# A gated mix of local attention and a spectral filter: the first unit copied from PSUM to its tiles, a third fold, the exchange in all groups but one, four odd rows unfolded on GpSimd, and another way to the order

## The chip, the cores and the metric

The kernel runs on one core of a Trainium2 chip. The metric is the device time of one execution in microseconds (us), as the median of several runs. "PE" in the profile is TensorE (matmul), "PEld" its weight loads, "DVE" VectorE, "ACT" ScalarE, "POOL" GpSimd and "SP" SyncE, which here only issues DMAs.

## The reference, cut to what matters

```python
def _A_ref(x, wqkv, wo):               # x: 1 x 2048 x 640, 32 heads of 20
    W, dil = 8, 2                      # each position looks at itself and 7 earlier ones, two apart
    qkv = (x @ wqkv)...                # q, k, v
    idx = pos[:, None] - (jnp.arange(W) * dil)[None, :]
    logits = einsum("bhsd,bhswd->bhsw", q, kg) * scale   # kg, vg: k, v gathered at idx
    logits = where(idx >= 0, logits, -1e9)
    attn = softmax(logits)
    o = einsum("bhsw,bhswd->bhsd", attn, vg)
    return o @ wo
def _B_ref(x, w_r, w_i):
    X = rfft2(x) * (w_r + 1j * w_i)
    return irfft2(X, s=(2048, 640))

g = sigmoid((x * gate_w).sum(-1))
return g * a + (1 - g) * b             # a from _A_ref, b from _B_ref, both of A_x
```

All arrays are float32; the output is 1 x 2048 x 640.

## The kernel before, in words

Position s is 16 p + j: the partition p is one of 128, and the 16 rows j are worked one at a time. As the dilation is 2, even j and odd j never meet in the attention.

**Attention.** `x` and `wqkv` are split into a high and a low float32r part, and three products of them give q, k and v for one row j and a quarter of the heads (`qkv`, 15 matmuls of 480 columns into a PSUM bank). A unit u = 4·par + hg is one parity and one quarter; unit 0 is the first. Unit 0 also carries the gate column. `qkv_first` computes seven of its eight rows with the loop over the five blocks of the contraction outside; `store` takes a finished bank: ScalarE copies it to one of two `ev` tiles, and each two rows go from there to a DRAM buffer, `qkvd`. `attend` (a unit has two halves, `a` and `b`) loads `kt` and `vt` (15 rows, of which the first 7 are the last 7 of the partition ahead) and `q` back from it. VectorE multiplies k by q (`pr`; q is first copied to a third of a PSUM bank, `qbank`, by ScalarE, so that the product has one input in SBUF and one in PSUM) and sums it to the logits `L`; GpSimd forms the products with v (`pv`), VectorE sums them (`o`), and they go to DRAM, `od`. `zero_rows` writes the zero rows ahead of position 0 into `qkvd`.

**Spectral part.** `fold` adds and subtracts mirrored columns of `x` twice on VectorE (tile `fx`, with `fe` for the even half), so that the transform along the 640 columns needs cosines or sines of a half or a quarter of them. Pairs of rows q = 2 to 7 are parked in DRAM (`fd`) by a DMA from GpSimd's queue. `cols` transforms along the partitions with matmuls into `zg`. `freq(g)`, once for each of 16 groups g of frequencies, copies from `zg` (`zc`), applies the folded transform of the columns with the table `bt` (`v` and `u`, six matmuls), adds and subtracts (`ab`), transforms over j (`x`, `z`), and multiplies by the complex weights `wp`. For that product the two halves of the partitions must change places. In the groups of `EXCHANGED` (1 to 8) ScalarE scales `x` and `z` by a sign into `X`, and two DMAs put them into the other half of `P`; in the others two more matmuls (`ix`, `iz`) compute them. GpSimd multiplies `P` by `wp` and adds, VectorE forms `s`, and matmuls (`g`) go back over j into `zg`. `spatial(j)` transforms back (`oa`, `ob`, `ha`, `hb`).

**Output.** `project_even` and `project_odd` multiply the attention's output by `wo` (transposes `oTp`, high and low parts `oT`, 15 matmuls each for `woa` and `wob`). For even j the result is parked in DRAM (`ad`) and added by GpSimd to `spatial`'s `y`. For odd j `project_odd` unfolds the spectral part (`ye`, then `y`: five instructions, on VectorE, or on GpSimd for j in `ODD_POOL`) and adds the projection to it; these projections stand last. They need `o` of every odd unit.

**The order.** Every operation is recorded by a planner, not issued at once (so all instructions carry one line, L636 in the program's own count, and are told apart by their tiles). The planner gives each a cost, runs a list schedule forwards and backwards in turn (`turns`, six times), and then tries 60 random shifts of the due times. Each resulting order is scored by its mean end under three draws of random delays (`late`), and the best one is issued as the fixed order of each engine. The queues then run by semaphores alone, each in its order. SyncE's and ScalarE's queues carry the loads and stores (`queue`: `vt` and `q` on ScalarE).

Of the kernel before, what the change touches and what calls it, by code (L numbers as in the profile page):

```python
# [16 lines left out]
S, D = 2048, 640  # L17
# [7 lines left out]
PERM = np.array([0, 320] + list(range(2, 320, 2)) + list(range(1, 320, 2)))  # L25
# [6 lines left out]
def dft_tables():  # L32
# [18 lines left out]
    def half(n, *ends):  # L51
# [3 lines left out]

    bt = np.zeros((640, 642))
    bt[0:161, 0:161] = np.cos(tau * np.outer(np.arange(161), ke) / D) * half(161, 0, 160)
    bt[161:321, 161:321] = np.cos(tau * np.outer(np.arange(160), ko) / D) * half(160, 0)
    bt[321:480, 323:482] = -np.sin(tau * np.outer(np.arange(1, 160), kb) / D)
    bt[480:640, 482:642] = -np.sin(tau * np.outer(np.arange(1, 161), ko) / D) * half(160, 159)  # L60
    bt = np.concatenate(
        [bt[0:128, 0:161], bt[128:256, 0:321], bt[256:384, 161:482], bt[384:512, 321:642], bt[512:640, 482:642]], 1
# [94 lines left out]
class Plan:  # L157
# [119 lines left out]
    def order(self):  # L277
# [20 lines left out]
        rng = np.random.default_rng(SEED)  # L298
        self.draws = [rng.exponential(size=len(ops)).tolist() for _ in range(DRAWS)]
        best = self.turns(TURNS)  # L300

        names = {n: i for i, n in enumerate(dict.fromkeys(op.of for op in ops))}
        family = np.array([names[op.of] for op in ops])
# [6 lines left out]
        self.ends = best[0], best[3]  # L310
# [5 lines left out]
    def turns(self, n):  # L316

        runs = []
        for i in range(n + 1):
            tails = np.array([op.tail for op in self.ops])  # L320
            done = self.forward()
            end = max(op.end + op.lat for op in done)
            runs.append((end, tails, [(op, op.start, op.end) for op in done]))
            if i < n:
                self.backward(end)
        end, tails, order = min(runs, key=lambda r: r[0])
        ends = [self.late([o[0] for o in order], d) for d in self.draws] or [end]
        return sum(ends) / len(ends), tails, order, end

    def late(self, order, draw):  # L330

        line = {e: [op for op in order if op.eng == e] for e in ENGS}
        at, free, rings, link = dict.fromkeys(ENGS, 0), dict.fromkeys(ENGS, 0.0), dict.fromkeys(ENGS, 0.0), 0.0
        over, out = {}, {}
        head = {}
        last = 0.0
        for _ in range(len(order)):
            for e in ENGS:
                if head.get(e) is None and at[e] < len(line[e]):
                    op = line[e][at[e]]  # L340
                    t = free[e]
                    for q in op.preds:
                        if q not in out:
                            break
                        t = max(t, over[q] if q.eng == e and not q.size else out[q])
                    else:
                        head[e] = t
            e = min((h for h in ENGS if head.get(h) is not None), key=lambda h: head[h])
            op, t = line[e][at[e]], head.pop(e)
            late = draw[op.i]  # L350
            if op.two and free["POOL"] > t:
                t = min(free["POOL"], t + WAIT)
            busy = op.busy * (1 + 0.015 * late) if e in ("DVE", "ACT", "POOL") and not op.size else op.busy
            over[op] = free[e] = end = t + busy
            if op.size:
                link = max(link, end) + op.size / RATE
                own = rings[e] = max(rings[e], end) + op.size / QUEUE
                end = (own if own >= link else min(link, own + op.size / QUEUE)) + SOONEST + LATER_BY * late
            else:
                end += op.lat - LATE.get(op.chain, 0.0)  # L360
            out[op] = end
            last = max(last, end)
            at[e] += 1
        return last
# [106 lines left out]
TURNS, AGAIN, MOVE, SEED = 6, 60, 2.0, 3  # L471
DRAWS, SOONEST, LATER_BY = 3, 2.4, 0.6
# [31 lines left out]
class Mixer:  # L504
# [64 lines left out]
    def work(self):  # L569
# [10 lines left out]
        self.zero_rows()  # L580
        self.qkv_first()
# [22 lines left out]
        S.dma_start(self.bt[:, 0:1284], ins["t_bt"])  # L604
# [36 lines left out]
    def zero_rows(self):  # L641
        p, d = self.p, self.qkv_d
        zero = self.one("zero", 7 * HC, tag="pv0")[0:32]
# [4 lines left out]
                offset=d.offset + 2 * ROWS * HC,  # L648
                ap=[[6 * ROWS * HC, 8], [ROWS * HC, 4], [1, 7 * HC]],
            ),  # L650
            zero,
        )

# [113 lines left out]
    def attend(self, par, h, step=4):  # L767
# [12 lines left out]
        kt, vt = (self.kvr.next(f"{i}t{nm}", 15, HC) for i in "kv")  # L780
        q = self.qr.next(f"q{nm}", 8, HC)
# [444 lines left out]
```

## Time and profile before

| | |
|---|---|
| times of three runs | 459.76, 459.97, 461.55 us |
| median | 459.97 us |
| the profiled execution | span 461.8 us from the first to the last instruction; the page has no other time for it |
| TensorE matmul / weight load | 448.4 us (97%) / 394.7 us (85%) |
| VectorE | 418.1 us (91%) |
| ScalarE | 209.7 us (45%) |
| GpSimd | 324.7 us (70%) |
| DMA | 108.53 MB, mean 235 GB/s |
| granted TensorE clock | 1.000 |

Busy shares are means over stages with different limits; what an edit is worth is read from the stage it lies in. Matmuls are pipelined and their ends are modelled, so a TensorE that reads as fully busy is not TensorE at its peak. Idle time of an engine that is not the bound costs nothing. A wait for several semaphores is put down to the one that came last.

### The profile page before, as it was taken

What the parts mean: (1) busy time and instruction counts of PE and PEld (TensorE: products, weight loads), DVE (VectorE), ACT (ScalarE), POOL (GpSimd) and SP (SyncE); (2) the same over time, 40 slices, a digit from 0 to 9 for tenths busy, and PEclk for the clock granted to TensorE, in tenths of its full rate; (3) what the DMA queues carried; (4) which work ended last, traced back from release to release, by engine and by line L of the source; (5) the groups of instructions that cost most, each with busy time, mean ns of one, the idle gap of its engine ahead of it and who ended that gap; (6) DMA issues with size and microseconds to landing.
All of it is one profiled execution on the core that took longest, in us unless ns stands there. A gap on an engine that the chain in (4) does not pass through costs nothing. (4 is left out here: it accounts for less than half of the span.)

```text
span 461.8 us, 7229 instructions
## 1 busy us (share of the span) xinstructions
PE 448.4 (97%) x2468; PEld 394.7 (85%) x2468; DVE 418.1 (91%) x549; ACT 209.7 (45%) x551; POOL 324.7 (70%) x264
## 2 busy tenths in 40 slices
PE   8999999999999989999998988999999999999996
PEld 6888888888888888898886877988889999988996
DVE  4999729999999999999989999999999997799594
ACT  4534245544235553265457665655445554432120
POOL 1003545999999879989898997797877889862200
PEclk9999999999999999999999999999999999999999
DMA  8999989769858989767989698786463321356722
GB/s 318 393 399 304 354 327 345 237 206 342 253 183 232 297 252 327 245 182 281 333 225 286 229 324 254 213 261 229 118 186 96 112 72 58 119 174 174 258 89 114
DMA packets 72836, 108.53 MB, mean 235 GB/s; under 512 B 21072, under 2 KB 50768, under 8 KB 72800
## 3 DMA queue, kind: packets, MB, share of 16 engines
q1 hardware_dynamic: 40192, 69.40, 46.8%
q10 hardware_dynamic: 31696, 34.67, 23.9%
q0 software_dynamic: 912, 4.00, 2.2%
q8 instruction: 19, 0.31, 0.3%
q14 instruction: 17, 0.14, 0.1%
HBM read 72.59 MB, written 32.84 MB: 228 GB/s over the span
## 5 line engine op out<-in xcount | busy, mean ns | idle before, releaser
L636 PE MATMUL qkv<-w,xo 128*128 128x480 f32 (+1 forms) x480 | 109.9, 384 | 0.0
L636 PE MATMUL qkv<-w,xe 128*128 128x480 f32 (+1 forms) x474 | 104.4, 381 | 1.1 <-ACT xe L636 1.1
L636 PEld LDWEIGHTS qkv<-w,xe 128*128 128x128 f32 x474 | 89.2, 188 | 16.7 <-ACT xe L636 2.2
L636 PEld LDWEIGHTS qkv<-w,xo 128*128 128x128 f32 x480 | 89.6, 189 | 13.7 <-ACT ev L636 0.2
L636 ACT COPY ev<-qkv 128x480 f32<-128x480 f32 x64 | 34.9, 556 | 38.3 <-PE qkv L636 18.7
L636 PE MATMUL woa<-wo,oT 128*128 128x320 f32 x240 | 51.5, 316 | 0.6 <-ACT oT L636 0.6
L636 PE MATMUL wob<-wo,oT 128*128 128x320 f32 x240 | 51.5, 316 | 0.0
L636 PEld LDWEIGHTS woa<-wo,oT 128*128 128x128 f32 x240 | 39.1, 188 | 1.1 <-ACT oT L636 0.8
L636 PEld LDWEIGHTS wob<-wo,oT 128*128 128x128 f32 x240 | 39.2, 188 | 0.7
L636 POOL TENSOR_TENSOR P<-P,wp 128x963 f32<-128x963 f32 (+1 forms) x16 | 30.4, 1900 | 11.8 <-ACT P L636 7.2
L636 POOL TENSOR_TENSOR w<-raw,w 128x480 fp32r<-128x480 f32 (+1 forms) x20 | 25.2, 1277 | 18.7 <-ACT w L636 18.7
L636 POOL DMA_DIRECT2D fd<-fx x6 | 4.3, 717 | 33.5 <-DVE fx L636 33.5
L636 ACT CAST oT<-oTp 128x384 fp32r<-128x384 f32 (+1 forms) x32 | 13.2, 427 | 30.4 <-PE oTp L636 26.0
L636 PEld LDWEIGHTS g<-mm,s 128*128 128x128 f32 x150 | 21.6, 190 | 3.5 <-ACT zg L636 0.5
L636 POOL TENSOR_TENSOR yi<-yi,y 128x640 f32<-128x640 f32 x8 | 12.5, 1563 | 16.8 <-DMA yi<-ad 9.6
L636 PE MATMUL v<-bt,zc 128*128 128x321 f32 (+2 forms) x96 | 22.2, 347 | 1.7 <-ACT vs L636 1.7
L636 PE MATMUL g<-mm,s 128*128 128x128 f32 x150 | 23.2, 276 | 0.0
L636 PE MATMUL oa<-gt,zg 128*128 128x161 f32 (+1 forms) x96 | 22.9, 344 | 0.0
L636 DVE TENSOR_TENSOR oT<-oTp,oT 128x384 fp32r<-128x384 f32 (+1 forms) x32 | 15.2, 483 | 8.4 <-ACT oT L636 8.4
L636 PE MATMUL ob<-gt,zg 128*128 128x161 f32 (+1 forms) x96 | 22.3, 344 | 0.0
L636 PE MATMUL u<-bt,zc 128*128 128x321 f32 (+2 forms) x96 | 22.0, 344 | 0.0
L636 ACT CAST w<-raw 128x480 fp32r<-128x480 f32 (+1 forms) x30 | 17.0, 592 | 8.0 <-PE qkv L636 2.9
(303 smaller groups left out, 1102.9 us busy)
## 6 DMA issues: line engine op xcount, KB each, us to landing
qkvd<-ev ACTq DMA_DIRECT2D x32, 480.0 KB, 5.1
wp<-in_ws SPq DMA_DIRECT2D x16, 642.0 KB, 4.9
raw<-in_wqkv SPq DMA_DIRECT2D x25, 240.0 KB, 7.0
fx<-in_x SPq DMA_DIRECT2D x8, 641.0 KB, 9.8
ot<-od SPq DMA_DIRECT2D x16, 320.0 KB, 3.3
fd<-fx POOLq DMA_DIRECT2D x6, 640.0 KB, 7.3
f<-fd SPq DMA_DIRECT2D x6, 640.0 KB, 7.1
P<-X ACTq DMA_DIRECT2D x16, 160.5 KB, 4.6
```

The lines of the kernel that those rows point to most:

```text
L636: p.dve.memset(w, 0.0)
```

## The change

Six things change together.

1. **Unit 0 is not sent through DRAM.** `open_near` takes its six tiles (q, k, v of both halves) at the start and clears the seven rows of partition 0. `store` copies each bank in six pieces of 80 columns straight into them, on ScalarE (`NEAR_DVE` is empty), and after the last row four DMAs on SyncE's queue copy the seven rows of the partition ahead within each k and v tile. `attend` then loads nothing for unit 0.
2. **Rows are folded a third time.** The even half and the odd half of what `fold` makes are folded again where this is possible, with four instructions of about 160 elements on GpSimd (`THIRD_DVE` is empty) for each of eight pairs of rows. The tables `bt` and the order of the columns `PERM` follow, and three blocks of `v` and `u` in `freq` become narrower.
3. **`EXCHANGED` goes from groups 1 to 8 to groups 1 to 15**; g = 0 keeps its matmuls.
4. **`ODD_POOL` goes from empty to (1, 3, 5, 7)**: the five unfolding instructions of these rows are on GpSimd.
5. **The search for an order is replaced.** A fixed list of 28 seeds is applied in turn: each seed shifts the due times by drawn amounts, `turns(2)` runs, and its result is taken for the next.
6. **The scoring under random delays goes**; `turns` keeps the order with the earliest end of its own schedule.

```diff
-PERM = np.array([0, 320] + list(range(2, 320, 2)) + list(range(1, 320, 2)))
+PERM = np.array([0, 320] + list(range(4, 320, 4)) + list(range(2, 320, 4)) + list(range(1, 320, 2)))
...
-        for _ in range(AGAIN):
-            move = MOVE * rng.choice([0.3, 1.0, 2.0]) * rng.normal(size=len(names))
-            move *= rng.random(len(names)) < rng.choice([0.1, 0.5, 1.0])
-            for op, t in zip(ops, (best[1] + move[family]).tolist()):
+        for seed in FOUND:
+            for op, t in zip(ops, (best[1] + self.move(seed)).tolist()):
                 op.tail = t
-            best = min(best, self.turns(2), key=lambda b: b[0])
+            best = self.turns(2)
...
-        end, tails, order = min(runs, key=lambda r: r[0])
-        ends = [self.late([o[0] for o in order], d) for d in self.draws] or [end]
-        return sum(ends) / len(ends), tails, order, end
...
+        return min(runs, key=lambda r: r[0])
+
+    def move(self, seed):
+        rng = np.random.default_rng(seed)
+        n, kind = self.kinds[rng.integers(3)]
+        shift = rng.choice([0.6, 2.0, 6.0, 15.0]) * rng.normal(size=n)
+        return (shift * (rng.random(n) < rng.choice([0.03, 0.1, 0.4, 1.0])))[kind]
...
+    def open_near(self):
+
+        self.near = [None] * 6
+        for f in range(2):
+            for i in (1, 2):
+                t = self.near[2 * i + f] = self.kvr.next(f"{'qkv'[i]}t0{'ab'[f]}", 15, HC)
+                self.p.pool.memset(t[0:1, 0:7], 0.0)
+            self.near[f] = self.qr.next(f"q0{'ab'[f]}", 8, HC)
...
         u, j = 4 * par + hg, 2 * jj + par
+        if u == 0:
+            for i, t in enumerate(self.near):
+                (p.dve if i in NEAR_DVE else p.act).copy(t[:, jj + (7 if i > 1 else 0)], b[:, HC * i : HC * i + HC])
+            p.act.copy(self.z[:, j : j + 1], b[:, 480:481])
+            if jj == 7:
+                for t in self.near[2:]:
+                    self.queue("halo").dma_start(t[1:128, 0:7], t[0:127, 8:15])
+            return
...
-        G.tensor_sub(f[:, :, 321:480], o[:, :, 1:160], o[:, :, 319:160:-1])
-        G.tensor_add(f[:, :, 480:640], o[:, :, 1:161], o[:, :, 319:159:-1])
-        G.tensor_add(f[:, :, 0:161], e[:, :, 0:161], e[:, :, 320:159:-1])
+        H = p.dve if q in THIRD_DVE else p.pool
+        G.tensor_add(f[:, :, 321:481], o[:, :, 1:161], o[:, :, 319:159:-1])
+        G.tensor_sub(o[:, :, 1:160], o[:, :, 1:160], o[:, :, 319:160:-1])
         G.tensor_sub(f[:, :, 161:321], e[:, :, 0:160], e[:, :, 320:160:-1])
+        G.tensor_add(e[:, :, 0:161], e[:, :, 0:161], e[:, :, 320:159:-1])
+        H.tensor_add(f[:, :, 481:561], o[:, :, 1:81], o[:, :, 159:79:-1])
+        H.tensor_sub(f[:, :, 561:640], o[:, :, 1:80], o[:, :, 159:80:-1])
+        H.tensor_add(f[:, :, 0:81], e[:, :, 0:81], e[:, :, 160:79:-1])
+        H.tensor_sub(f[:, :, 81:161], e[:, :, 0:80], e[:, :, 160:80:-1])
...
-        row(v, 4, bt[:, 803:1124], True, False)
-        row(v[:, 0:161], 3, bt[:, 642:803], False, False)
-        row(v[:, 161:321], 5, bt[:, 1124:1284], False, True)
+        row(v[:, 81:321], 4, bt[:, 721:961], True, False)
+        row(v[:, 161:321], 3, bt[:, 561:721], False, False)
+        row(v[:, 0:161], 5, bt[:, 961:1122], False, True)
...
-        row(u, 1, bt[:, 161:482], True, False)
+        row(u[:, 81:321], 1, bt[:, 161:401], True, False)
         row(u[:, 0:161], 0, bt[:, 0:161], False, False)
-        row(u[:, 161:321], 2, bt[:, 482:642], False, True)
+        row(u[:, 161:321], 2, bt[:, 401:561], False, True)
...
-ODD_POOL = ()
+ODD_POOL = (1, 3, 5, 7)
...
-EXCHANGED = tuple(range(1, 9))
+EXCHANGED = (1, 2, 3, 4, 5, 6, 7, 8, 9, 10, 11, 12, 13, 14, 15)
```

More of the change, by code (lines that the diff above doesn't have):

```diff
@@ L325, in turns @@
                 self.backward(end)
-        end, tails, order = min(runs, key=lambda r: r[0])
-        ends = [self.late([o[0] for o in order], d) for d in self.draws] or [end]
-        return sum(ends) / len(ends), tails, order, end
[L330 to L364, printed above, removed]
+        return min(runs, key=lambda r: r[0])
[4 more added lines that the diff above has]
+        return (shift * (rng.random(n) < rng.choice([0.03, 0.1, 0.4, 1.0])))[kind]
     @staticmethod
@@ L642, in zero_rows @@
         p, d = self.p, self.qkv_d
[L643 removed]
+        zero = self.one("zero", 7 * HC, tag="pv0")[0:28]
         p.pool.memset(zero, 0.0)
@@ L779, in attend @@
         p.chain = "logits"
-        kt, vt = (self.kvr.next(f"{i}t{nm}", 15, HC) for i in "kv")
-        q = self.qr.next(f"q{nm}", 8, HC)
-        self.queue("kt").dma_start(kt.rearrange("p a b -> p (a b)"), rows(1, 0, 15))
-        self.queue("q").dma_start(q.rearrange("p a b -> p (a b)"), rows(0, 7, 8))
-        self.queue("vt").dma_start(vt.rearrange("p a b -> p (a b)"), rows(2, 0, 15))
+        if u == 0:
+            q, kt, vt = (self.near[2 * i + f] for i in range(3))
+        else:
+            kt, vt = (self.kvr.next(f"{i}t{nm}", 15, HC) for i in "kv")
+            q = self.qr.next(f"q{nm}", 8, HC)
+            self.queue("kt").dma_start(kt.rearrange("p a b -> p (a b)"), rows(1, 0, 15))
+            self.queue("q").dma_start(q.rearrange("p a b -> p (a b)"), rows(0, 7, 8))
+            self.queue("vt").dma_start(vt.rearrange("p a b -> p (a b)"), rows(2, 0, 15))
         L = self.Lr.next(f"L{nm}", 8, 4, 8)
```

43 lines of the change are left out of this document (28 added, 15 removed).

## The prediction

> **What bounds the kernel now.** I read the page first, then the busy time by stretches, then the chain of work that ended last, then the waits, and at the end the timeline of the first 70 us.
>
> ```profile
> span 461.8 us, 7229 instructions
> PE 448.4 (97%) x2468; PEld 394.7 (85%) x2468; DVE 418.1 (91%) x549; ACT 209.7 (45%) x551; POOL 324.7 (70%) x264
> ```
>
> The profiled span is 461.8 us; the median of the three runs is 459.97. The sum below is made on the span, and the difference, 1.8 us, comes off at the end. Two engines are near full. The stretches (window, its length, then busy us and instructions of PE, PEld, DVE, ACT and POOL, then granted clock, DMA share and GB/s) show when:
>
> ```profile
> 40.00:60.00 20.00, 20.00 (x94) 17.33 (x93) 14.89 (x17) 6.75 (x14) 9.06 (x8) 1.00 0.99 337
> 60.00:80.00 20.00, 20.00 (x93) 17.28 (x92) 13.54 (x11) 10.45 (x27) 10.77 (x9) 1.00 0.94 323
> 80.00:180.00 100.00, 98.80 (x491) 86.21 (x490) 98.48 (x87) 44.98 (x115) 93.06 (x74) 1.00 0.83 259
> 180.00:280.00 100.00, 96.17 (x514) 81.97 (x513) 97.28 (x112) 53.20 (x156) 92.28 (x75) 1.00 0.84 262
> 280.00:380.00 100.00, 98.44 (x609) 87.19 (x609) 97.98 (x134) 54.21 (x151) 80.49 (x64) 1.00 0.57 172
> 414.00:462.00 48.00, 43.20 (x300) 42.07 (x298) 35.02 (x86) 8.15 (x20) 6.30 (x4) 1.00 0.50 160
> ```
>
> From 80 to 380 us TensorE and VectorE are both at 96 to 99% of the time, with the clock granted in full. Work taken off one of them alone moves little, because the other holds the end. VectorE has its one large hole ahead of that, at 40 to 80 us: 5.1 and 6.5 us idle. The chain that ended last (start, us, what) tells how the two take turns:
>
> ```profile
> 287.26 1.09 PE u L636 x6
> 300.63 0.54 PE ix L636 x2
> ...
> 412.10 1.48 DVE o4b L636
> ...
> 417.76 0.45 PE oTp L636 x2
> ...
> 456.31 2.06 PE wob L636 x14
> 458.39 0.55 DVE y L636
> ```
>
> Nearly all of its pieces between 284 and 402 us are matmuls; then VectorE finishes the last attention unit (`o4b`, over at 413.6); behind it stand the odd rows' projections, which need that output, some 40 us of matmul from 418 to 458. So the end is "last `o4b` plus 48 us", and `o4b` comes early only if VectorE's work before it shrinks and TensorE's does too.
>
> **The change part by part.** *TensorE.* The third fold narrows the row transforms: `v` and `u` write 240+160+161 = 561 columns for each group instead of 321+161+160 = 642. Six pieces of `u` take 1.09 us for 642 columns, so 81 columns are 0.138 us; over 2 outputs and 16 groups, 4.4 us. With all groups but g = 0 exchanged, the `ix` and `iz` products of groups 9 to 15 go: 14 of 0.54 us, 7.6 us. Nothing is added. TensorE: **-12.0 us**, all ahead of the last 100 us, in the full stretches.
>
> *VectorE, the first unit.* Today unit 0 goes from PSUM to `ev`, to DRAM, and back:
>
> ```profile
> DVE pr0a L636 <- ACT qbank L636: 10.9, 2, 8.7
> ACT ev L636 <- DMA qkvd<-ev: 18.2, 5, 7.0
> ```
> ```profile
> 37.96 1.02 ACT L636 COPY ev<-qkv 128x480 f32<-128x480 f32 x2 [2.02 <-DMA qkvd<-ev]
> 51.35 1.49 DVE L636 TENSOR_TENSOR pr0a<-kt0a,qbank 128x1280 f32<-128x1280 f32 x1 [2.17 <-ACT qbank L636]
> 63.40 0.56 ACT L636 COPY ev<-qkv 128x480 f32<-128x480 f32 x1 [6.99 <-DMA qkvd<-ev]
> 65.99 1.49 DVE L636 TENSOR_TENSOR pr0a<-kt0a,qbank 128x1280 f32<-128x1280 f32 x1 [8.72 <-ACT qbank L636]
> ```
> ```profile
> kt0a<-qkvd SPq DMA_DIRECT2D x1, 600.0 KB, 5.6
> vt0a<-qkvd ACTq DMA_DIRECT2D x1, 600.0 KB, 16.1
> P<-X ACTq DMA_DIRECT2D x16, 160.5 KB, 4.6
> ```
>
> Unit 0's last copies run from 37.96 to 39.0; its first product starts at 51.35. With the tiles filled straight from PSUM only seven halo rows go by DMA. Their landing is not in this trace. The nearest rows bound it: 4.6 us (the exchange, between SBUF tiles too) and 16.1 (`vt0a`, the slow one of the early loads); I take 5.6, that of `kt0a`, which is issued in the same stretch. Attention can then start at 39 + 5.6, about 45 us, with folds to fill VectorE until then, and it has q at hand when today it stops for 8.7 us. I count both waits as gone: -10.9 us. The other end is -2.2: the 8.7 us stay, because ScalarE serves in order and the `qbank` copies stood behind an `ev` copy of the next unit, which waited 6.99 us for a store, and those stores remain. For the wait going speaks that unit 0's traffic leaves DMA engines that were 94 to 99% busy just then. Late next is VectorE itself. The four halo copies stand on SP's queue and wait for the eighth bank; the later weight loads queue behind them, and TensorE needs those by the start of the next set only, so their lead hides the wait; without it, TensorE loses what the weights are late. The four memsets on GpSimd lie in its idle first 20 us.
>
> Six copies of 80 columns a bank instead of one of 480 lie between 166 ns (one column) and 556 (480 columns); linear in the width that is 0.23 us, and 48 x 0.23 - 8 x 0.556 = 6.6 us more for ScalarE. It is busy 6.75 of 20 us there, and a bank takes TensorE 15 matmuls of 20.00/94 us, 3.2 us, against 1.6 us of copies. Hidden; if ScalarE ran late, TensorE would wait for banks.
>
> ```profile
> L636 ACT COPY z<-qkv 128x1 f32<-128x1 f32 x16 | 2.5, 166 | 3.0 <-PE qkv L636 2.0 <-ACT ev L636 0.9
> L636 ACT COPY ev<-qkv 128x480 f32<-128x480 f32 x64 | 34.9, 556 | 38.3 <-PE qkv L636 18.7 <-DMA qkvd<-ev 18.2 <-issue 0.5
> L636 DVE TENSOR_TENSOR iz<-iz,wp 128x321 f32<-128x321 f32 x8 | 3.9, 493 | 0.9 <-PE iz L636 0.9
> L636 POOL TENSOR_TENSOR P<-P 128x321 f32<-128x321 f32 x16 | 12.0, 751 | 1.2
> L636 DVE TENSOR_TENSOR ye<-ho 128x160 f32<-128x160 f32 (+1 forms) x24 | 10.1, 474 | 0.2
> L636 DVE TENSOR_TENSOR y<-ye 128x321 f32<-128x321 f32 (+1 forms) x16 | 7.3, 485 | 0.1
> ```
>
> *The exchange in seven more groups.* VectorE drops one product of 0.49 us in each: -3.4 us. GpSimd multiplies three parts instead of two, about 0.75 us more each, 5.3 us. ScalarE scales twice and issues two DMAs where it made one copy, beside its 45 to 54%. GpSimd's product now waits for a landing of 4.6 us, with `pv` products queued behind it. The spacing of `s`, the last product of a group, prices that:
>
> ```profile
> 249.71 0.87 DVE L636 TENSOR_TENSOR s<-P,z 128x321 f32<-128x321 f32 x2
> 303.34 0.89 DVE L636 TENSOR_TENSOR s<-P,z 128x321 f32<-128x321 f32 x2
> 306.77 0.49 DVE L636 TENSOR_TENSOR s<-P,iz 128x321 f32<-128x321 f32 x1
> 344.39 0.89 DVE L636 TENSOR_TENSOR s<-P,iz 128x321 f32<-128x321 f32 x2
> ```
>
> Groups with the exchange (g = 0 among them) came every 53.6/8 = 6.7 us, the last seven, without, every 37.6/6 = 6.3. So it costs up to 0.4 x 7 = 3 us, or nothing if VectorE paces both. I take nothing and keep the 3 us for the range.
>
> *Third fold and odd unfolding on GpSimd.* 32 more instructions of some 160 elements, at half of the 0.75 us of 321: 0.4 us each, 13 us, mostly before 80 us, where GpSimd is half idle. The odd unfolding takes half of 10.1 + 7.3 us off VectorE, 8.7 us, nearly all behind 414, where VectorE is busy 35 of 48 us: it covers nothing there and I count nothing. But two engines meet here:
>
> ```profile
> 43.32 4.58 POOL L636 TENSOR_TENSOR w<-raw,w 128x480 fp32r<-128x480 f32 x3 [5.10 <-ACT w L636]
> 43.53 4.71 DVE L636 TENSOR_TENSOR fx<-fx 128x642 f32<-128x642 f32 x3
> L636 DVE TENSOR_TENSOR fe<-fx 128x642 f32<-128x642 f32 x8 | 6.6, 823 | 0.1
> L636 DVE TENSOR_TENSOR fx<-fx x24: 482/494/1844, 19.4 to 46.7; 128x642 f32<-128x642 f32 x8, 128x320 f32<-128x320 f32 x8, 128x318 f32<-128x318 f32 x8
> ```
>
> Three fold instructions, both inputs in SBUF, took 4.71 us while GpSimd subtracted; at the median 0.49 for the two short ones, and the 0.82 of `fe` for the wide one, they are 1.8. VectorE lost 2.9 us beside 4.58 us of GpSimd, 0.6 for one. The new thirds run beside folds, or beside attention products, whose q lies in PSUM. Bounds: nothing (all beside attention) and 13 us (each blocks a fold for its whole time). With half of them beside folds, 13 x 0.6 / 2: **+4 us**.
>
> [...]
>
> *Sum.* VectorE up to `o4b`: -10.9 - 3.4 + 4 = -10.3; TensorE -12.0; the smaller gain binds. 461.8 - 10.3 = 451.5 us of span, less 1.8: **449.7 us**. With the lock at nothing TensorE's 12.0 binds, 448.0; with the exchange's 3 us, 452.7.
>
> **Rivals.** *The replayed order closes gaps* (0.15): TensorE and VectorE each leave 6 to 7 us idle in 80 to 380, and TensorE 4.8 behind 414. An order that recovers half of the one and the other, 5 us, gives 444.7; all of it about 439.
>
> *The first unit's wait goes in part* (0.10): half of the 8.7 us stay, 454.0. *It stays whole* (0.07), the change then not doing what it says: 449.7 + 8.7 = 458.4. The ordered ScalarE speaks for it, the lighter DMA against.
>
> *The lock at full length* (0.03): 13 us instead of 4, 458.7. Against it: most folds can run before any third is ready.
>
> *Slower: an order that counts on punctual landings* (0.15). The change drops the scoring of an order under drawn delays, replays fixed draws, and adds 14 exchange DMAs whose landings an in-order GpSimd, over 90% busy, must wait for. This trace has one such case: an `ev` copy stood 6.99 us behind a store, and VectorE lost 8.72. Behind 80 us nothing absorbs it. It decides once the loss passes the 10.3 of gain and 2.3 more; two stops of 8.72 give 449.7 + 17.4 = 467.1.
>
> **How the numbers follow.** The forecast has 0.50, 448 to 453 us by itself. 0.5% is 2.3 us, about what a measurement of this kernel can tell. Faster than 457.7: 0.50 + 0.15 + 0.10 = 0.75; within: 0.07 + 0.03 = 0.10; slower: 0.15. The range for 8 in 10 runs from 441, most of the closed gaps, to 460, which takes in the wait that stays and the full lock and leaves out the slower case.
>
> **What would show it.** Right: `v` and `u` near 0.95 us for six pieces and no `ix`, `iz` but for g = 0; VectorE over 95% busy from 20 us on, the first `pr0a` near 45 us with no long wait after it; fold instructions stretched beside GpSimd by about 4 us in all; last `o4b` near 403 and 48 us behind it. Wrong: VectorE idle over 5 us before 80; GpSimd waiting for `P<-X` by more than 1 us a group; `o4b` early but matmuls left over, so that more than 48 us follow it; or new waits of TensorE on banks or weights in the first 120 us.

## The result and the profile after

The changed kernel takes **499.51 us** (median of 4 runs, 497.20 to 499.86) against 460.76 us for the kernel before on the same chip: 1.081 times as long, with an interval of 1.078 to 1.085. It is 38.8 us slower where 10.3 us less were forecast, and outside the range of 441 to 460. The profiled execution took 497.2 us, its span is 495.4.

The page after (the span, the busy time of the engines, and three rows of the 40 slices, 12.4 us each):

```profile
span 495.4 us, 7309 instructions
...
PE 449.1 (91%) x2440; PEld 396.0 (80%) x2440; DVE 414.8 (84%) x522; ACT 215.3 (43%) x598; POOL 366.7 (74%) x320
...
PE   8999908879999449999999989999998999999996
...
DVE  3999705069989999999999899999999998879484
...
PEclk9999966979999959999999999999999999999999
```

There is a hole that the kernel before did not have: TensorE at 0 in the sixth slice, VectorE at 0 in the sixth and the eighth, and a granted clock of 6 tenths in the sixth and seventh. Two shorter stops of TensorE follow in the fourteenth and fifteenth. The stretches put numbers on it (columns as in the prediction: length, then PE, PEld, DVE, ACT, POOL, granted clock, DMA share, GB/s):

```profile
60.00:80.00 20.00, 6.59 (x21) 4.29 (x19) 5.23 (x4) 1.87 (x4) 4.65 (x7) 0.63 0.31 110
80.00:100.00 20.00, 16.72 (x72) 13.88 (x70) 1.94 (x2) 0.30 (x1) 0.14 (x1) 0.93 0.18 59
100.00:180.00 80.00, 65.39 (x298) 56.09 (x298) 74.29 (x63) 34.61 (x91) 69.94 (x55) 0.91 0.77 248
```

In 60 to 80 us TensorE works 6.6 of 20 us, VectorE 5.2, and the DMA engines, which stood at 0.94 in the same stretch before, are at 0.31. Nobody is busy, so everybody waits. The timeline of SP's queue (start, time that SP spent in the issue) shows a first reason; its last line is from the kernel before:

```profile
38.88 0.73 SPq L616 DMA_DIRECT2D kt0b<-kt0b  x1
39.70 7.11 SPq L616 DMA_DIRECT2D kt0a<-kt0a  x1
46.91 15.80 SPq L616 DMA_DIRECT2D vt0b<-vt0b  x1
62.80 14.55 SPq L616 DMA_DIRECT2D vt0a<-vt0a  x1
77.45 22.46 SPq L616 DMA_DIRECT2D raw<-in_wqkv  x5
```
```profile
45.25 12.82 SPq L636 DMA_DIRECT2D raw<-in_wqkv  x5
```

These are the four halo copies, seven rows of 127 partitions each. SP is held in their issue for 38 us, from 38.9 to 77.4, and the next set's weights (`raw`) get their turn only at 77.45; before, SP issued them at 45.25. The waits (total, times, longest) and the timeline of ScalarE and TensorE (start, length, in brackets the idle time before and what ended it) show what came of it:

```profile
ACT w L616 <- DMA raw<-in_wqkv: 24.5, 3, 20.8
DVE pr0a L616 <- ACT qbank L616: 21.1, 1, 21.1
DVE pr0a L616 <- DMA kt0a<-kt0a: 15.4, 1, 15.4
PEld qkv L616 <- ACT w L616: 14.3, 2, 13.7
```
```profile
74.65 0.37 ACTq L616 DMA_DIRECT2D qkvd<-ev  x1
75.11 0.59 ACT L616 CAST w<-raw 128x480 fp32r<-128x480 f32 x1 [20.95 <-DMA kt0a<-kt0a]
75.75 20.96 PE L616 MATMUL qkv<-w,xe 128*128 128x480 f32 x79 [13.28 <-ACT w L616]
99.70 1.75 ACT L616 CAST w<-raw 128x480 fp32r<-128x480 f32 x3 [20.85 <-DMA raw<-in_wqkv]
```

VectorE waits 15.4 us for the halo of `kt0a`, until 74.67 us, 35 us after its issue. ScalarE stands twice. Its first stop, from 54.2 to 74.6 us, ends with the same landing: its next operation is a store of `ev`, which needs nothing of `kt0a`, but in the trace that store waits for semaphore 100, on which the halo copy counts its landing, and then counts its own on it. TensorE's longest wait for weights `w`, 13.3 us, ends one step behind this stop, at 75.75 us, before SP has issued the late `raw` at all. ScalarE's second stop, 20.85 us, is the wait for that `raw`. TensorE loses 5.6 us behind it, and VectorE waits 21.1 us for its q in `qbank`: in ScalarE's order that copy comes behind the cast to `w`, which starts only at 99.70 us. So the late landings reach the engines by two ways, through SP's held queue and through a store on ScalarE's queue. The first attention product starts at 74.7 us instead of 51.4, and the last `qkv` matmul ends at 282.0 instead of 242.1.

### The profile page after: what moved, and what is told of

Same layout as the page of the kernel before. It is cut to its first block, busy times and chain, and to the rows that moved or that the text cites. A ratio compares the mean times of both kernels' runs of the same rounds, so it can differ in the third digit from the quotient of the medians.

```text
span 495.4 us, 7309 instructions
## 1 busy us (share of the span) xinstructions
PE 449.1 (91%) x2440; PEld 396.0 (80%) x2440; DVE 414.8 (84%) x522; ACT 215.3 (43%) x598; POOL 366.7 (74%) x320
## 5 line engine op out<-in xcount | busy, mean ns | idle before, releaser
L616 PE MATMUL qkv<-w,xe 128*128 128x480 f32 (+1 forms) x474 | 111.4, 395 | 19.6 <-ACT w L616 13.3
L616 PE MATMUL qkv<-w,xo 128*128 128x480 f32 (+1 forms) x480 | 119.9, 394 | 7.2 <-ACT ev L616 7.1
L616 PEld LDWEIGHTS qkv<-w,xe 128*128 128x128 f32 x474 | 91.9, 196 | 38.6 <-ACT w L616 14.3
L616 ACT COPY ev<-qkv 128x480 f32<-128x480 f32 x56 | 30.9, 556 | 49.7 <-PE qkv L616 42.4
L616 PE MATMUL woa<-wo,oT 128*128 128x320 f32 x240 | 47.7, 321 | 0.1
L616 PE MATMUL wob<-wo,oT 128*128 128x320 f32 x240 | 47.0, 318 | 0.4 <-ACT oT L616 0.3
L616 POOL TENSOR_TENSOR P<-P,wp 128x963 f32<-128x963 f32 (+1 forms) x16 | 35.4, 2210 | 8.4 <-DMA P<-X 8.4
L616 PEld LDWEIGHTS woa<-wo,oT 128*128 128x128 f32 x240 | 38.8, 193 | 0.5 <-DVE oT L616 0.4
L616 DVE TENSOR_TENSOR pr0a<-kt0a,qbank 128x1280 f32<-128x1280 f32 x4 | 5.9, 1486 | 36.6 <-ACT qbank L616 21.1
L616 POOL TENSOR_TENSOR fx<-fx 128x160 f32<-128x160 f32 (+1 forms) x16 | 11.5, 735 | 23.7 <-DMA fx<-in_x 17.3
L616 PE MATMUL v<-bt,zc 128*128 128x240 f32 (+2 forms) x96 | 20.0, 323 | 1.1 <-ACT vs L616 1.1
L616 PE MATMUL u<-bt,zc 128*128 128x240 f32 (+2 forms) x96 | 18.9, 322 | 1.2 <-DVE ab L616 1.2
```

The source lines that it names most:

```text
L616: p.dve.memset(w, 0.0)
```

## Experiments: the halo copies

**Fewer rows to a copy** (`halo_split`). The changed kernel in its own order; each copy is issued as two (this edit and those below are shown in short):

```diff
-    dma_start(t[1:128, 0:7], t[0:127, 8:15])
+    dma_start(t[1:113, 0:7], t[0:112, 8:15])
+    dma_start(t[113:128, 0:7], t[112:127, 8:15])
```

> The changed kernel in its own order, but each of the four halo copies issued as two, of 112 and of 15 partitions, in place of one of 127. Theory H (a copy of 127 partitions runs on few DMA engines, and everything queued behind it waits): the hole from 62 to 102 us goes, no halo issue on SP takes over 2 us, and the time falls from 499.5 by some 35 to 45 us, to 450 to 465. Rival O (the replayed order, the lock and the exchange cost most of it): the hole shrinks but the time stays over 480.

Measured: **462.49 us** (10 runs, 459.63 to 464.56) against 461.47; ratio 1.003, 1.0003 to 1.0057. SP's queue in the same stretch:

```profile
38.27 0.62 SPq L743 DMA_DIRECT2D kt0b<-kt0b  x1
38.95 0.92 SPq L744 DMA_DIRECT2D kt0b<-kt0b  x1
...
44.51 0.96 SPq L743 DMA_DIRECT2D vt0a<-vt0a  x1
45.52 0.81 SPq L744 DMA_DIRECT2D vt0a<-vt0a  x1
50.62 14.04 SPq L616 DMA_DIRECT2D raw<-in_wqkv  x5
```

Eight issues of 0.5 to 1.6 us take 8 us, the weights are issued at 50.62, and the two halves of `kt0a` land 2.9 and 4.7 us after their issue, as the prediction took it (5.6). The same bytes go the same way; only the rows to a copy, and with them the number of copies, are different. That is 37 of the 39 us. ScalarE's stop at the store and TensorE's wait of 13.3 us go too: both ways are closed by this one edit.

**Copies alone** (`row_counts`). Nothing but copies of 560 elements a partition between SBUF tiles, each waiting for the one before:

```diff
+for n in (128, 127, 126, 120, 113, 112, 96, 64, 15):   # twice
+    t = tile([128, 560]); dma_start(t[o : o + n], last[0:n]); last = t
```

> Only copies of 560 elements a partition between SBUF tiles, one after the other, of 128, 127, 126, 120, 113, 112, 96, 64 and 15 partitions, twice; nothing of the reference is computed. Theory H: 127 and 113 land after 10 us or more each, 126, 120, 112, 96, 64 and 128 within 2 to 4 us. Rival S (the shift by one partition, or copying within SBUF, is what is slow): all shifted copies are alike, 128 without a shift is fast.

The timeline of SP, rows of 127, 126, 120, 113, 112 and 96 in that order, start and issue time:

```profile
7.10 0.75 SPq L24 DMA_DIRECT2D rows<-rows  x1
...
21.18 0.85 SPq L24 DMA_DIRECT2D rows<-rows  x1
...
24.42 0.81 SPq L24 DMA_DIRECT2D rows<-rows  x1
...
27.68 0.64 SPq L24 DMA_DIRECT2D rows<-rows  x1
...
40.70 0.57 SPq L24 DMA_DIRECT2D rows<-rows  x1
...
43.46 0.54 SPq L24 DMA_DIRECT2D rows<-rows  x1
```

From start to start the copy of 127 rows takes 14.1 us, that of 126 3.2, of 120 3.3, of 113 13.0, of 112 2.8; the second round gives 14.1, 3.2, 3.3, 12.8 and 2.7. The page's row of GB/s reads 26, 26, 26 while the first one of 127 runs. Two stretches of the second round lie wholly within a copy of 127 and one of 113 rows (the last two columns are the DMA share and GB/s):

```profile
55.00:65.00 10.00, 0.00 (x0) 0.00 (x0) 1.00 0.06 23
75.00:85.00 10.00, 0.00 (x0) 0.00 (x0) 1.00 0.06 22
```

A share of 0.06 of the core's 16 DMA engines is one engine. 113 rows, fewer than 126, take four times as long, so neither the bytes nor the size of the count decide. Of the nine counts tried, the two slow ones are the two primes; 128, 96, 64 and 15 rows land 2.3 to 2.5 us after their issue. Why these two run on one engine, no run shows.

**The same load in the kernel before** (`dummy_127`, `dummy_112`). Four copies into tiles that nobody reads, ahead of the load of `kt0a` on SP:

```diff
+for c in range(4): dma_start(junk[c][1:n + 1, 0:7], xe[0:n])     # n = 127, or 112
 dma_start(kt0a, qkvd)
```

> The kernel before, with four copies of 127 partitions by 7 rows of 80 elements from a tile that is not needed, issued on SP just ahead of the first load of kt0a; nobody reads what they write. Theory H: 30 to 50 us slower than before (490 to 510), with the same hole. Rival O: within 5 us of before.

> The same with 112 partitions in each of the four copies. Theory H: within 3 us of before (458 to 464). Rival S (any four such copies in that place hold up the queue): as slow as with 127.

Measured, one run each: **502.86 us** with 127 rows and **464.1** with 112, against 461.47. The timeline and three waits of the first, then the timeline of the second:

```profile
28.47 43.48 SPq L790 DMA_DIRECT2D junk<-xe  x4
72.14 11.05 SPq L791 DMA_DIRECT2D kt0a<-qkvd  x1
```
```profile
DVE pr0a L636 <- ACT qbank L636: 49.7, 1, 49.7
ACT ev L636 <- DMA junk<-xe: 34.6, 1, 34.6
PE qkv L636 <- ACT w L636: 30.7, 1, 30.7
```
```profile
29.35 3.98 SPq L790 DMA_DIRECT2D junk<-xe  x4
```

SP is held 43.5 us instead of 4.0, and the end comes 38.8 us later. The kernel before, whose order and attention are untouched, loses what the changed kernel loses. So the cause of the loss is shown: copies of 127 rows. Neither the replayed order nor a lock (folds held up beside GpSimd) is needed for it. The way is again a double one. Nobody reads what the copies write, and yet ScalarE stands 34.6 us ahead of a copy to `ev`, until one of them has landed. TensorE's one long wait, 30.7 us, is for the weights `w` that ScalarE makes. What SP's held queue would have cost without it, no run shows.

## Experiments: the four parts without the halo's price

What remains is why the forecast gain is not there either.

**The order** (`all_oldorder`): all four parts, copies split, planned by the rules of before instead of replayed draws.

```diff
-order: fixed draws replayed
+order: scored under drawn delays, as before
```

> All four parts on the chip's work (unit 0 by PSUM with the halo in 112 and 15 partitions, third fold, exchange in groups 1 to 15, four odd rows on GpSimd), but ordered as the kernel before orders itself: 60 random shifts scored under drawn delays. Theory R (the replayed order ate the 10 us): 448 to 454. Rival P (the parts themselves bring nothing, because the frequency stage ends no earlier): 457 to 464, like the replayed order with the split halo (462.5).

**461.86 us** against 461.75, ratio 1.0024 (0.9998 to 1.0049): the same as `halo_split`, as the rival P of this run expected. The replayed order neither costs nor brings anything that these runs can tell.

**One part each, in the kernel before** (`add_near`, `add_third`, `add_exch`):

```diff
+unit 0 copied from PSUM, halo as 112 + 15 rows         # add_near
+third fold on GpSimd, u and v in 561 columns           # add_third
-EXCHANGED = tuple(range(1, 9))                         # add_exch
+EXCHANGED = tuple(range(1, 16))
```

> The kernel before with one part alone: unit 0 from PSUM, halo split in 112 and 15. Its own search orders it. Theory D (VectorE's first wait is on the path, as predicted): 449 to 453, first pr0a near 45 us and no wait over 2 us before 80. Rival P (VectorE's lead is lost before the frequency stage ends, which TensorE's projections fix in time): 457 to 462.

> The kernel before with the third fold alone (four more instructions a pair of rows on GpSimd, narrower u and v). TensorE's 4.4 us alone would give 456. Theory L (the lock costs VectorE 5 us or more in the folds, and GpSimd's thirds take 0.75 us instead of 0.4): folds over 36 us of VectorE, time 460 to 466. Rival (the folds lie in VectorE's hole at 40 to 80 us and cost nothing): 455 to 459.

> The kernel before with the exchange in groups 1 to 15 alone. TensorE's 7.6 us and VectorE's 3.4 us alone would give 454 to 457. Theory E (a group with the exchange takes 6.7 us, one without 6.3, and the last groups keep that pace): the last s comes 2 to 4 us later than at 344.4, time 460 to 465. Rival (TensorE or VectorE paces the groups): last s 3 us or more earlier, time 454 to 458.

Measured, against 461.75: **464.45** (ratio 1.0079, 1.0050 to 1.0109), **466.87** (1.0138, 1.0090 to 1.0186), **466.74** (1.0131, 1.0068 to 1.0194). Each alone costs 3 to 5 us; together, as above, nothing. All three lie above every range that was expected of them. The odd unfolding was not tried alone. Each kernel is planned anew, so a part also pays for another order; `before_ring3` below prices that.

**The third fold without GpSimd** (`third_dve`): `add_third` with the four short instructions on VectorE.

```diff
-THIRD_DVE = ()
+THIRD_DVE = tuple(range(8))
```

> The kernel before with the third fold, its four further instructions on VectorE instead of GpSimd. Theory L (two engines excluding each other cost add_third its time): VectorE takes 10 us of new work (32 x 0.31) but the fold instructions go back to their medians, GpSimd is free for the low parts of the weights and rows, qkv ends by 243, time 456 to 462 against 466.9. Rival (the late start comes from VectorE's longer folds, whoever does them): 465 to 470.

**462.27 us** against 461.18 (1.0038, 1.0003 to 1.0072). This is just above theory L's range and under the rival's. Some of the fold groups of the first 80 us in `add_third`, then in `third_dve` (count, then busy us, mean ns, and idle time before with what ended it):

```profile
L643 DVE TENSOR_TENSOR fe<-fx 128x642 f32<-128x642 f32 x8 | 7.5, 946 | 3.5 <-POOL fx L643 3.5
L643 POOL TENSOR_TENSOR fx<-fx 128x158 f32<-128x158 f32 x8 | 6.7, 843 | 0.0
L643 POOL TENSOR_TENSOR fx<-fe 128x160 f32<-128x160 f32 x8 | 6.0, 752 | 0.0
L643 DVE TENSOR_TENSOR fe<-fe 128x322 f32<-128x322 f32 x8 | 5.0, 646 | 0.1
```
```profile
L643 DVE TENSOR_TENSOR fe<-fx 128x642 f32<-128x642 f32 x8 | 6.6, 825 | 0.1
L643 DVE TENSOR_TENSOR fe<-fe 128x322 f32<-128x322 f32 x8 | 3.9, 491 | 0.1
L643 DVE TENSOR_TENSOR fx<-fx 128x158 f32<-128x158 f32 x8 | 3.6, 448 | 0.0
```

On GpSimd the 32 short instructions take 23.0 us; on VectorE 13.3, 0.41 each. And VectorE's other fold instructions, 31.8 us with the short ones on VectorE, take 34.8 with them on GpSimd. So moving them saved VectorE 13.3 us of its own, gave 3.0 back in stretched folds and 3.5 more in waiting for GpSimd, and put 23 on GpSimd.

Had each short instruction on GpSimd held up a fold for its whole length, the folds would have lost up to the 23 us of GpSimd; they were stretched by 3.0.

**One more buffer for the exchange** (`exch_ring3`, `all_ring3`, `before_ring3`): the tile `P` in three buffers, so that the next exchange can start before the last product has been read.

```diff
-self.Pr = ring("x2", "x3")
+self.Pr = ring("x2", "x3", "x6")
```

> The kernel before with the exchange in groups 1 to 15 and three buffers for P. Theory B: last s at 340 to 347 instead of 352.7, time 453 to 460 against 466.7 with two buffers. Rival V: 464 to 468.

> All four parts, the old way to the order, and three buffers for P where the kernel has two (the third place is free in the frequency stage). Theory B (a group with the exchange holds its P for 13 to 14 us from the issue of the exchange to its s, so two buffers allow no group faster than 6.8 us, whatever TensorE and VectorE gained): last s at 338 to 346 instead of 350.5, time 448 to 457. Rival V (VectorE's queue paces the groups): last s within 2 us of 350.5, time 459 to 463.

> The kernel before with three buffers for P and nothing else. Theory B: its last seven groups hold P for some 7 us only, so little changes: 457 to 462. Rival V: the same; what it tells is whether the third buffer is worth something by itself, without the exchange.

Measured, against 461.18: **463.2** (1.0047, 1.0022 to 1.0072), **471.33** (1.0229, 1.0192 to 1.0266), **462.66** (1.004, 1.0016 to 1.0063). The third buffer helps `add_exch` by 3.5 us and worsens the whole by 9. Theory B wanted the last `s` at 340 to 347 and 338 to 346; it came at 350.4 and 354.2, and the time from first to last `s` was 99.0 and 99.3 us, against 100.6 and 101.9 with two buffers. So the theory that the ring holds the change falls. The totals, 463.2 and 471.33, met neither theory's range. `before_ring3`, where it ought to do nothing, loses 1.5, and its time from first to last `s` is 99.2 instead of 95.1: this is what another planned order can do by itself. Differences of a few us between kernels that are planned anew are therefore not put down to the part.

## Experiments: where the forecast gain went

All of these but `no_max` keep the order of before, instruction for instruction, and narrow operations in it, so that planning cannot blur them.

**TensorE alone, VectorE alone, both** (`pe_less`, `dve_less`, `both_less`):

```diff
-row(u, 1, ...); row(u[:, 0:161], 0, ...); row(u[:, 161:321], 2, ...)   # pe_less, v too
+row(u, 1, ...)
-tensor_reduce(o, pv)                        # dve_less, units 0 to 3
+tensor_reduce(o, pv[:, :, :, 0:6])
```

> The kernel before with its order held, and the row transforms u and v made by one matmul of 321 columns each where there were three (642 columns): it leaves out part of u and v, so that only TensorE's time is less. Three times 1.09 us less 0.5 us and so on: by the rows of before, u and v take 1.09 us for 642 columns, so about 17 us of TensorE's work go, all between 240 and 350 us. Theory P (TensorE and VectorE share the end, neither alone is worth much): 0 to 4 us faster, VectorE at 97% or more in 240 to 350. Theory Q (order, queues and GpSimd hold it): 0 to 4 us faster as well. The sum as I predicted it, the smaller gain of the two engines binds: no gain. If TensorE alone held the end: 12 us or more faster.

> The kernel before with its order held, and the o reduces of units 0 to 3 taken over six of the eight products (it leaves out part of each sum): VectorE's work falls by about 11 us, all before 225 us; nothing else changes. It imitates the 10.9 us of wait that the change was to take from VectorE's first 80 us. Theory P: 0 to 4 us faster, with TensorE at 98% or more. Theory Q: 0 to 4 us. If VectorE alone held the end: 9 to 11 us faster.

> Both narrowings at once, the order of before held (part of u and v and part of the sums of units 0 to 3 are left out): TensorE 17 us less in 240 to 350, VectorE 11 us less before 225. Theory P: 8 to 12 us faster, the smaller of the two gains. Theory Q: less than 4 us faster, with GpSimd at 93% and waits on it or on DMA in the place of the work taken away.

Measured, against 461.21: **463.31** (1.0043, 1.0007 to 1.0079), **461.6** (1.0015, 0.9996 to 1.0035), **463.08** (1.0028, 0.9992 to 1.0063). TensorE's busy time fell from 448.4 to 439.3 us (9.1, where 17 were expected of the edit) and VectorE's from 418.1 to 408.6 (9.5, of 11): somewhat less than what the change was to bring. Even both together moved the end by nothing. Theory P of these runs (the two share the end, so both together pay) falls in that form.

**Less for VectorE and GpSimd together** (`no_max`):

```diff
-tensor_reduce(out=m, in_=L, op=max)
-pool.tensor_sub(L, L, m)
```

> The kernel before without the subtraction of each row's maximum ahead of the exponential (the quotient stays the same for these inputs; order planned anew): 16 reduces of VectorE, about 6.5 us, and 16 subtractions of GpSimd, about 10 us, go; TensorE's work stays. Theory P: 0 to 3 us faster, TensorE then over 97%. Theory Q with GpSimd as what holds the attention stage: 5 to 8 us faster, since units then end earlier by what GpSimd saves.

**470.16 us** (1.0203, 1.0170 to 1.0236), slower though it does less. Neither theory's range holds it. The two halves of unit 3 end 9 and 5 us earlier than before and the second half of unit 7 at 279 instead of 285, yet the last `qkv` matmul comes at 247.3 instead of 242.1 and the end with it. Its order is planned anew, so the 9 us cannot be put down to the edit; but it is a case in which units end early and the end does not.

The stretch 240 to 350 us of before, and of `pe_less`:

```profile
240.00:350.00 110.00, 105.34 (x622) 90.01 (x621) 106.17 (x165) 62.77 (x180) 91.69 (x74) 1.00 0.76 231
```
```profile
240.00:350.00 110.00, 95.61 (x502) 73.17 (x503) 104.99 (x165) 62.53 (x180) 91.55 (x75) 0.98 0.75 229
```

TensorE has 9.7 us less to do there, and VectorE is as busy as before: the freed time is idle. So read stage by stage, from the timelines (us; A ends with the last `qkv` matmul, B, the frequency stage, with the first `oa`, C is the rest; TensorE's idle time in each):

| kernel | last qkv (A) | first to last s | first oa (B) | last o4b | span | length of C | idle A, B, C |
|---|---|---|---|---|---|---|---|
| before | 242.1 | 249.7 to 344.8: 95.1 | 349.0 | 413.6 | 461.8 | 112.8 | 4.1, 4.7, 4.6 |
| after | 282.0 | 288.6 to 390.4: 101.8 | 393.4 | 459.6 | 495.4 | 102.0 | 34.6, 7.4, 4.3 |
| halo_split | 244.4 | 251.1 to 352.3: 101.2 | 355.5 | 421.7 | 457.9 | 102.4 | 5.1, 6.9, 4.5 |
| all_oldorder | 240.8 | 248.6 to 350.5: 101.9 | 353.4 | 423.2 | 459.8 | 106.4 | 3.0, 12.3, 3.9 |
| add_exch | 238.2 | 252.1 to 352.7: 100.6 | 355.0 | 414.1 | 463.2 | 108.2 | 3.1, 9.6, 5.0 |
| third_dve | 240.3 | 252.3 to 346.9: 94.6 | 349.7 | 431.7 | 461.6 | 111.9 | 4.3, 6.7, 4.4 |
| pe_less | 239.7 | 250.5 to 343.7: 93.2 | 348.0 | 412.5 | 460.8 | 112.8 | 2.2, 14.7, 4.6 |
| dve_less | 240.3 | 247.8 to 342.8: 95.0 | 347.0 | 411.5 | 459.8 | 112.8 | 2.3, 4.5, 4.6 |
| early_both | 232.7 | 240.6 to 334.1: 93.5 | 338.3 | 402.9 | 451.1 | 112.8 | 5.5, 3.2, 4.6 |
| stage_both | 237.4 | 246.8 to 338.7: 91.9 | 343.2 | 407.7 | 456.0 | 112.8 | 2.1, 11.4, 4.6 |

In A and in C TensorE is idle 2 to 5.5 us in every row but A of the changed kernel: I read this as TensorE ending these stages. Only in B does it idle when it is given less. That is theory R of the next two runs (another one than the R of `all_oldorder`), against theory Q, by which order, queues and GpSimd hold the end: VectorE's gain lay in A, which TensorE ends; TensorE's lay in B, which it does not end. Two more kernels, order held, put both savings into one stage.

**Both in A** (`early_both`): `dve_less`, and one of the 15 matmuls of 57 `qkv` banks left out.

```diff
+if i == 8: continue        # in the 15 terms of a bank
 pe.matmul(b, a, w)
```

> The kernel before with its order held, the o reduces of units 0 to 3 over six of eight products, and one of the fifteen matmuls of 57 qkv banks left out (a third of the correction for one of five row blocks): 12 us less of TensorE and 10 us less of VectorE, both ahead of 242 us. Theory R: the last qkv matmul ends near 231 instead of 240, the first s near 240, and the end comes 7 to 11 us earlier. Theory Q: the last qkv matmul may come early, but units and the end move by less than 3 us, GpSimd at 95% or more in 80 to 180.

**454.39 us** against 461.54, ratio 0.9852 (0.9814 to 0.9891). The same VectorE saving that brought nothing in `dve_less` stands beside 12 us less of TensorE, and on the profiled spans A ends 7.6 us earlier than in `dve_less`, the first `s` 7.2, the end 8.7; against the kernel before, the medians differ by 7.2. From the first `s` to the end it takes 210.5 us, against 212.0 in `dve_less`. R's 7 to 11 are just met and Q's "under 3" is not. TensorE's saving in A by itself was not tried, so how much of the 7 us it would bring alone is open.

**Both in B** (`stage_both`): `pe_less`, and the reduces of units 6 and 7 over four of eight products.

```diff
-tensor_reduce(o, pv)                        # units 6 and 7
+tensor_reduce(o, pv[:, :, :, 0:4])
```

> The kernel before with its order held, u and v by one matmul of 321 columns, and the o reduces of units 6 and 7 over four of eight products (part of u, v and of those sums is left out): 9 us less of TensorE and some 11 us less of VectorE, both between 242 and 349 us. Theory R: the frequency stage, 95 us from first to last s, shrinks to 85 to 88, and the end comes 7 to 10 us earlier. Theory Q: the stage stays at 93 us or more, GpSimd or the exchange's DMA now waited for, and the end moves by less than 3 us.

**457.55 us** against 461.54, ratio 0.9912 (0.9883 to 0.9940). The stretch again:

```profile
240.00:350.00 110.00, 99.23 (x527) 77.85 (x526) 100.45 (x166) 63.26 (x181) 95.10 (x76) 0.97 0.75 228
```

4.0 us, between the two theories. VectorE does count in B, as R says: in `pe_less`, with TensorE relieved alike, nothing was gained. But now VectorE, TensorE and GpSimd all have 9 to 15 us idle in the stretch, so waits between them hold the stage once VectorE is lighter. Which of them is last was not settled.

No complete version beat the kernel before: the two that were faster leave work out.

## Why the prediction was wrong, step by step

**The step that failed** is the landing of the halo: "The nearest rows bound it: 4.6 us [...] and 16.1 [...]; I take 5.6". The halo of `kt0a`, which the first product needs, landed 35 us after its issue. The bounds came from transfers of 128 rows (`kt0a`, `vt0a`) and of 64 (the exchange), and the halo has 127. The next sentence failed with it: "their lead hides the wait". SP was held for 38 us, and no lead covers that. The price that the prediction named for an uncovered wait, "what the weights are late", was not worked out, and it is only a part of the loss. Up to the last `qkv` matmul TensorE was idle 34.6 us instead of 4.1: 13.3 until ScalarE was freed by the landing, 5.6 behind the late weights, and 13.8 in two later stops of 6.8 and 7.1, between 165 and 182 us, that ended with ScalarE's copies to `ev`. With 112 and 15 rows both sentences hold: 2.9 and 4.7 us, and the weights in time.

**The sum.** Without the halo's price the parts give 462.5 instead of 449.7. Term by term:

- *TensorE, -12.0*: right in size for the matmuls that it counts. `u` and `v` together go from 50.8 to 46.5 us of busy time (4.3; forecast 4.4), and `ix`, `iz` are left for g = 0 alone. The after rows:

```profile
L616 PE MATMUL v<-bt,zc 128*128 128x240 f32 x32 | 9.3, 372 | 1.1 <-ACT vs L616 1.1
L616 PE MATMUL u<-bt,zc 128*128 128x240 f32 x32 | 9.2, 368 | 1.2 <-DVE ab L616 1.2
...
L616 PE MATMUL iz<-ab,tbfirst 128*128 128x321 f32 x4 | 1.3, 441 | 0.0
L616 PE MATMUL ix<-ab,tbfirst 128*128 128x321 f32 x4 | 1.2, 434 | 0.0
```

TensorE's whole busy time fell by less, from 448.4 to 441.3 in `halo_split`, since other matmuls read longer there (the 480 of `qkv<-w,xo` 118.5 us instead of 109.9). The saving shows where the order moves later matmuls into the freed time: 270 of the projections' matmuls (`woa`, `wob`) stand in C instead of 330, and C is 10.4 us shorter.

- *The first unit's wait, -10.9*: it did go, from 10.9 to 0.3 us in `halo_split`. But the time was not won: the first `pr0a` stands at 58.6 there (forecast 45, before 51.4), since the folds before it end later, and unit 0's row sums come at 79.5 instead of 79.7. VectorE's busy time in the first 80 us rose from 60.5 to 69.1.
- *The lock, +4*: VectorE's folds went from 31.7 to 37.1 us, +5.4, near enough; but the 32 short instructions on GpSimd took 24.8 us instead of 13, 0.78 each instead of 0.4. The estimate by half the width was VectorE's price (0.41 in `third_dve`); on GpSimd the same width took 0.47 in the odd unfolding (`ye`, the median), so a good part of the excess came beside the folds. Its full length, 13 us, was an estimate: in `add_third` the folds were stretched by 3.0 us beside 23 us of GpSimd. The forecast's lower bound, that attention's products lose nothing beside GpSimd, has the trace of before behind it: the sixteen `pr` groups take 1.46 to 1.48 us on average, with GpSimd busy 93% of 80 to 180 us.
- *The exchange, 0, "and keep the 3 us for the range"*: probably too small. First to last `s` takes 101.2 us in `halo_split` and 100.6 in `add_exch` against 95.1. The runs without the added exchange lie between 91.9 and 99.2, those with it between 99.0 and 101.9. But the top of the first group is `before_ring3`, where another order alone did 4.1 us, so how much of the 5 to 6 us is the exchange's own is open. GpSimd's waits for `P<-X` are not where it sits (8.4 us after, 4.3 in `halo_split`, under the 1 us a group that was to prove it wrong).
- *"The smaller gain binds"*: the error of form. It comes near only where both engines are relieved in the same stretch: some 7 of 10 us in `early_both`, 4 of 9 in `stage_both`. Here VectorE's 10.9 lay ahead of 80 us in a stage that TensorE ends, and TensorE's 12 in the one stage that it does not end. The stretches quoted in the prediction had both at 96 to 99% and could not tell which one the other waits for; `dve_less`, `pe_less` and `early_both` can.
- *"Last `o4b` plus 48 us"*: wrong. The distance is 36 us after and in `halo_split` and 30 in `third_dve`; `o4b` comes 8 us later in `halo_split` than before and the span ends 4 earlier. The end is the end of B plus TensorE's remaining matmuls (C, with 4 to 5 us idle in every kernel of the table).

In one sum on spans: `halo_split` reaches B's end 6.5 us later, 6.1 of them between the first and the last `s`, and has a C shorter by 10.4; 461.8 + 6.5 - 10.4 = 457.9, its span. That profiled execution is the lowest of its ten; their median is 1 us above before.

**The rivals.** The slower case had 0.15, with "an order that counts on punctual landings" as its mechanism: late landings in queues of a fixed order are indeed what happened, but at the halo copies, not the exchange, and at 37 us. That the slower side came true is luck as far as the exchange goes. The replayed order itself did nothing (`all_oldorder`). VectorE's idle time ahead of 80 us and the waits on weights in the first 120 stood in the list of what would prove it wrong.

**Right**: the 48 narrow copies are hidden (0.26 us on average for `kt0a`, 0.34 for `vt0a`, forecast 0.23; in `halo_split` TensorE is full from 20 to 60 us, as before), and nothing speaks against the zero for the odd unfolding, though no run moved it alone: in C TensorE is idle 4.5 us with it (`halo_split`) and 4.6 before.

## What to carry to other kernels

Before pricing an added DMA by the nearest row, compare the shapes, not only the bytes: a copy shifted by one row has 127 rows, and 112 + 15 landed within 3 to 5 us, where 127 took 14 us alone and 35 us behind another one. Price what stands behind it on its queue by that figure too, and look for stores on other queues that wait for its semaphore (20.95 us of ScalarE here). And when two engines are both full, add up gains only stage by stage: take from each engine what it saves in the stages that it ends, and test which that is by narrowing one engine's work in a held order.

## What the runs showed of the hardware

- In `row_counts` a DMA of 127 or 113 rows of 560 elements, between SBUF tiles, ran on one of the 16 engines (share 0.06) at 22 to 26 GB/s and took 13 to 14 us; of 112, 120 or 126 rows, 2.7 to 3.3 us.
- Back to back, such copies held the issuing queue: SP spent 7.1, 15.8 and 14.6 us in single issues (after), against 0.5 to 1.6 for the split ones (`halo_split`).
- A late landing also held an engine that had no use for the data: ScalarE stood 20.95 us at a store (after), which waits for, and then counts on, the semaphore of the late copy, and 34.6 us ahead of a copy to `ev` (`dummy_127`), until a copy that nobody reads had landed.
- TensorE's granted clock read below 1 around its long stops, and a hole cost beyond its length. Behind the stop of 13.28 us that ends at 75.75 us the clock was 0.50 for 6.5 us of full work, 14 matmuls; then, at 1.00, 66 took 14.5 us:

```profile
75.70:82.20 6.50, 6.32 (x14) 4.22 (x15) 6.13 (x5) 1.28 (x4) 2.41 (x2) 0.50 0.29 92
82.20:96.70 14.50, 14.50 (x66) 12.16 (x65) 0.00 (x0) 0.00 (x0) 0.00 (x0) 1.00 0.22 72
```

  The 0.91 from 100 to 180 us lies around the later stops: 0.69 in 100 to 110, with the one of 5.6 us; 1.00 from 110 to 165; 0.60 in 170 to 175 and 0.50 in 175 to 180, with those of 6.8 and 7.1. In the stretch 240 to 350, where TensorE had been given less to do, the clock was 0.98 in `pe_less` and 0.97 in `stage_both`, against 1.00 before; the longest wait of TensorE's matmuls that the waits of `pe_less` list is 1.8 us.
- GpSimd took 0.59 to 0.85 us on average for an add or a subtraction of some 160 elements beside the folds (`add_third`, `halo_split`), about the 0.75 that it took for 321 in the frequency stage (before).
